# A bias turned by four vector transposes instead of one matrix transpose, in a layernorm, GELU and two-matmul kernel

## The chip, the core and the metric

The kernel runs on one core of a Trainium2 chip. The core has a matrix engine (PE, with its weight loads PEld), a vector engine (DVE), a scalar engine (ACT), a third elementwise engine (POOL) and an engine that issues transfers (SP). Each engine works through its own list of instructions in order and waits on semaphores that other engines and transfers raise. On-chip memory (SBUF) and the accumulation banks (PSUM) have 128 partitions. The metric is the device time of one execution in microseconds (us), less is better.

## What is computed

```python
B, S, D, F = 1, 2048, 1024, 3584          # bf16 inputs
y = layernorm(x)                          # over the last axis, eps 1e-5
h = gelu(y @ w1 + b1)                     # tanh form; b1 has F entries
out = h @ w2 + b2
```

The change touches only how `b1` is brought into the layout in which it is added.

## The kernel before

**Tiles and blocks.** The 2048 rows of x form 16 tiles of 128 rows, in four blocks of 512 (`TB`). The first product is made transposed: one "row" r of 128 columns of w1 times a block gives a 128 x 512 tile of h transposed, in one PSUM bank, by eight matmuls of 128 x 512 (one for each slice dt of D). There are 28 such rows (`FT`). GELU on ACT reads the bank, adds the bias and writes `hT_sb`. The bias must therefore lie with one h column per partition: `b1_sb` is 128 x 28, and row r uses its column r as the per-partition bias (L396 to L399). In memory b1 is a line of 3584 numbers, so it is loaded as 28 rows of 128 (`b1r_sb`) and has to be turned.

**The bias before.** ACT issues the load of b1 and then the load of the first piece of w1, "w0" (`issue`, L216 to L226). `pe_b1` (L520) turns `b1r_sb` with one PE transpose of 28 x 128 into bank "1_1", and `put_b1` (L524) copies it from there to `b1_sb` on ACT. Both stand ahead of all other PE and ACT work except the 25 warm-up matmuls (`warm`, L458) and the first two issues of ACT; the call is at L561. The first matmul that writes bank "1_1" waits for this copy (`bank_read`).

**The start of the first block.** Tiles 0, 1 and half of 2 are turned on PE as they arrive (`pe_T_one`, L326: six slices of tile 0, two of tile 1, two of tile 0, six of tile 1), copied out by ACT (`put_copy`, L336), and multiplied without being normalised ("raw"). Eight rows ("the wave", `R_WAVE`) are open at once in eight PSUM banks, and their matmuls (`pe_wave`, L377) come in the order in which pieces of w1 land. Tile 3 is normalised by DVE and joins last, with 56 + 8 narrow matmuls row by row (L621 to L624).

**The repairs.** Since tiles 0 to 2 went in raw, each wave row is repaired in PSUM on DVE: an operation a (`ops_fix`, L545) that adds the mean's part and an operation b (L548) that multiplies by one over the deviation. GELU of row r on ACT waits for b of row r and for "b1c", the bias copy. In between, DVE makes centred copies of the raw tiles in four operations `ctr0` to `ctr3` (L538): two before the repairs, two after those of the first two rows. The order is written by hand in L628 to L630: a0, a1, b0, b1, ctr2, ctr3, then a and b of rows 2 to 7. DVE's list ends there for the wave; then come scalings of rows 8 to 27 (L412) mixed with the layernorm and the transposes of later blocks, in an order that a planner with estimated due times works out (L668 to L683).

**What waits for the repairs.** Rows 8 to 27 of the first block (`mm1_row`, L404) reuse banks: row 8 takes the bank of row 0, row 9 that of row 1, and so on through five banks, and then row 13 takes the bank "t" of row 7. Each waits for the GELU of the row that held the bank. Rows 8 and up also read the centred tiles, two slices for each `ctr`.

**Other lines.** L469 turns the statistics with transposes of 32 x 96 in groups of four, which step through the 32-partition quarters; L492 and L479 turn half a tile and a whole tile in 32 x 32 blocks, L310 turns later tiles in pieces of 32 x 256; L475 spreads the turned statistics over the partitions (ACT); L608 takes column sums (ACT).

Of the kernel before, what the change touches and what calls it, by code (L numbers as in the profile page):

```python
# [7 lines left out]
BF16 = mybir.dt.bfloat16  # L8
# [4 lines left out]
P = 128  # L13
# [83 lines left out]
def bass_standalone__mixer_channel_mlp__prompt_kernel(  # L97
# [11 lines left out]
    F = w1.shape[1]  # L109
    NT = ST // P  # L110
    DT = D // P
    FT = F // P
# [34 lines left out]
    with ExitStack() as es:  # L147
        sb = lambda name, shape, dt: es.enter_context(nc.sbuf_tensor(name, shape, dt))
# [6 lines left out]
        hT_sb = sb("hT_sb", [P, FT, TB], BF16)  # L155
        o_sb = sb("o_sb", [P, NOB, D], BF16)
        b2_sb = sb("b2_sb", [P, D], BF16)
        b1r_sb = sb("b1r_sb", [FT, P], BF16)
        b1_sb = sb("b1_sb", [P, FT], F32)
        ident = sb("ident", [P, P], BF16)  # L160
        ones = nc.const_aps.tensor(1.0, [P, P], BF16)
# [18 lines left out]
        pe = _Prog("s_pe")  # L180
        act = _Prog("s_act")
# [10 lines left out]
        def dma(dst, src, sig, nbytes, waits=()):  # L192
            dma_q[0].op(lambda e, dst=dst, src=src: e.dma_start(dst, src), waits=waits, sig=sig, sem="d_" + sig, inc=16)
            dma_bytes[0] += nbytes
            est[sig] = DMA_T0 + dma_bytes[0] / DMA_BYTES_PER_US

        def load_x_tile(i):
            dma(x_sb[:, i, :], xf[i * P:(i + 1) * P, :], f"x{i}", P * D * 2)
            x_ev[i] = (f"x{i}", f"x{i}")
# [7 lines left out]
        def load_w1(ci):  # L207
            j0, j1, a, b = w1_chunks[ci]
            dma(w1_sb[:, j0:j1, a:b], w1v[:, j0:j1, a:b], f"w1c{ci}", (j1 - j0) * P * (b - a) * 2)
            w1_issued.add(ci)  # L210
# [5 lines left out]
        def issue(item):  # L216
            if item == "b1":
                dma_q[0] = act
                dma(b1r_sb[:, :], b1.rearrange("(t p) -> t p", p=P), "b1", F * 2)
                dma_q[0] = sp  # L220
            elif item[0] == "x":
                load_x_tile(int(item[1:]))
            elif item[0] == "w" and int(item[1:]) < len(w1_chunks):
                dma_q[0] = act if item == "w0" else sp
                load_w1(int(item[1:]))
                dma_q[0] = sp  # L226

        act.op(lambda e: e.preload_act_table(ACT.Gelu_apprx_tanh))
        for item in SP_FIRST_LOADS:
            issue(item)  # L230
# [8 lines left out]
        for b in range(2, NB):  # L239
# [4 lines left out]
                sig="ident")  # L244
# [70 lines left out]
        def dve_put(o):  # L315
            dve.op(o[0], waits=o[1], sig=o[2])

        pe_t = [T_PE_START]
        bank_read = {}
        bank_of = {"t": ps_t[:, 0, :], "2_0": ps_2b[:, 0, :], "2_1": ps_2b[:, 1, :], "1_1": ps_1b[:, 1, :], "1_2": ps_1b[:, 2, :], "1_3": ps_1b[:, 3, :],  # L320
                   "1_4": ps_1b[:, 4, :]}
# [151 lines left out]
        def put_row_spread(k, q0, q1):  # L473
            for q in range(q0, q1):
                act.op(lambda e, q=q: e.copy(out=row_b(k)[32 * q:32 * (q + 1)], in_=row_b(k)[0:32]),  # L475
                       waits=[f"row_q{k}"], sig=(f"row_{k}" if q == 3 else None))
# [40 lines left out]
                       sig=("te3" if (tq, q) == todo[-1] else None))  # L517
            yT_ev[3] = ["te3"] * DT

        def pe_b1():  # L520
            pe.op(lambda e: e.transpose(out=bank_of["1_1"][:, 0:FT], in_=b1r_sb[:, :], identity=ident[0:FT, 0:FT]),  # L521
                  waits=["ident", "b1"], sig="b1t")

        def put_b1():  # L524
            act.op(lambda e: e.copy(out=b1_sb[:, :], in_=bank_of["1_1"][:, 0:FT]), waits=["b1t"], sig="b1c")
            bank_read["1_1"] = "b1c"

        row_b = lambda k: row_r[:, :, :].rearrange("p (t k) s -> p t k s", k=2)[:, :, k, :]
        raw_cols = lambda bank, c0: unit_bank(bank)[:, c0:c0 + len(RAW) * P].rearrange("p (t s) -> p t s", t=len(RAW))
# [2 lines left out]
        def ops_centre():  # L532
            res = []
            for k, (j0, j1) in enumerate(zip(CENTRE[:-1], CENTRE[1:])):
                xt, ct = [yT_sb[:, k, j0:j1, ycol(RAW[0]):ycol(RAW[0]) + len(RAW) * P].rearrange(
                    "p j (t s) -> p j t s", t=len(RAW)) for k in (0, ybuf(0))]
                m = row_b(0).unsqueeze(1).to_broadcast([P, j1 - j0, len(RAW), P])
                res.append((lambda e, xt=xt, ct=ct, m=m: e.tensor_tensor(out=ct, in0=xt, in1=m, op=ALU.subtract),  # L538
                            ["row_0"], f"ctr{k}", 0.95))
            return res  # L540
# [15 lines left out]
        ctr = ops_centre()  # L556
        seq = st[0] + st[1][:1] + turn_2() + st[1][1:] + st[2] + turn_m[:2] + st[3] + turn_m[2:] + nm[3] + moves_3() + turn_r + ctr[:2]
        for o in seq:
            dve_put(o)

        pe_b1()  # L561
        put_b1()
        T_BANKS = (("t", "2_0"), ("2_1", "1_4"), ("t", "2_0"))
        for t, j in [(0, j) for j in range(N_AHEAD)] + [(1, j) for j in range(GROUPS[1])] + [
                (0, j) for j in range(N_AHEAD, DT)] + [(1, j) for j in range(GROUPS[1], DT)]:
# [40 lines left out]
        def put_cs(c0, c1, src):  # L606
            mine = [r for r in range(R) if c0 <= bank_col(wave[r][0]) < c1]
            act.op(lambda e, c0=c0, c1=c1, src=src: e.mul(ncs[:, c0:c1].unsqueeze(2), src, -1.0),  # L608
                   waits=[f"raw_{r}" for r in mine], sig=f"cs{c0}")
            for r in mine:  # L610
                cs_ev[r] = f"cs{c0}"
# [5 lines left out]
        put_cs(NB1, NB1 + NB2, ps_2[:, 0:NB2, one0:one0 + 1])  # L617
        put_cs(NB1 + NB2, R, ps_tf[:, one0:one0 + 1].unsqueeze(1))
        put_row_spread(1, 3, 4)
        fixes = []  # L620
        for r in range(R):  # L621
            for dt in range(DT):
# [3 lines left out]
            act_gelu(r, 0, TPB, wave[r][0], f"fx_b{r}", f"g_0_{r}")  # L626
            hT_row[(0, r)] = f"g_0_{r}"
        (a0, b0), (a1, b1_) = fixes[:2]  # L628
        for o in [a0, a1, b0, b1_] + ctr[2:] + [o for f in fixes[2:] for o in f]:
            dve_put(o)  # L630
        for t in RAW:
            yT_ev[t] = [f"ctr{k}" for k, (j0, j1) in enumerate(zip(CENTRE[:-1], CENTRE[1:])) for _ in range(j0, j1)]
# [37 lines left out]
        while ci < len(crit) or fi < len(fill):  # L670
# [5 lines left out]
            if take_crit:  # L676
                rdy, o, _ = crit[ci]
                ci += 1
            else:
                rdy, o, _ = fill[fi]  # L680
# [46 lines left out]
```

## Time and profile before

| what | value |
|---|---|
| median of three runs | 396.22 us (395.76 to 396.69) |
| the profiled execution | 396.51 us |
| its span, first to last instruction | 395.3 us |
| granted PE clock, mean | 1.000 |
| PE busy | 390.9 us of the span, 1916 matmuls |
| DVE busy | 162.7 us, 339 instructions |
| ACT busy | 87.1 us, 145 instructions |
| bias load, issue on ACT | 0.81 us, for 0.63 us, 7 KB |
| w0 load, issue on ACT | 1.47 us, for 0.37 us, 128 KB, 3.1 us to landing |
| PE transpose of the bias (L521) | one, 202 ns, at 3.58 us |
| ACT copy of the bias (L525) | one, 182 ns, at 3.82 us |

Times of single instructions are given from the start of the span. A line of the timeline gives start, length, engine, source line, operation, result and operands, shapes and count; instructions of one kind are merged, so that a length can cover several, and in brackets stand the idle time ahead and what ended it. A line of the list of groups gives the count, the busy time, the mean in ns, and the idle time before. Matmuls overlap in their records: the distance between starts is the pace, not the length.

### The profile page before, as it was taken

To read this page: it belongs to the slowest core of one execution; us is meant where nothing else is said; L and a number is where in the kernel's file an instruction comes from. 1 tells how busy PE (TensorE), PEld (TensorE's weight loads), DVE (VectorE), ACT (ScalarE), POOL (GpSimd) and SP (SyncE) were. 2 spreads that over 40 slices of the span, in tenths; PEclk is the share of its full clock that TensorE was granted. 3 is DMA by queue.
4 is the path that set the end of the run, shared out by engine and by line. 5 is a ranking of instruction groups with operands and counts; after the bars stand their busy time and mean duration, and the time that the engine had idled before them with its cause. 6 is when DMAs were issued, how large, how long until landed. Compare 5 with 4: busy or idle time off the path is not lost.

```text
span 395.3 us, 4562 instructions
## 1 busy us (share of the span) xinstructions
PE 390.9 (99%) x1916; PEld 185.8 (47%) x1950; DVE 162.7 (41%) x339; ACT 87.1 (22%) x145; POOL 14.0 (4%) x69
## 2 busy tenths in 40 slices
PE   9999999999999999999999999999999999999998
PEld 8744444444444444444444444444444444444444
DVE  6998889998999306987100000001100000001011
ACT  5655420000134332000023443000003334400000
POOL 5201000011001100000000000000000000000000
PEclk9999999999999999999999999999999999999999
DMA  7999930000000000000000000000000000000000
GB/s 273 375 385 387 387 139 27 15 27 14 28 0 0 2 0 0 28 27 15 27 13 2 0 0 2 13 13 28 25 15 15 0 2 0 0 15 27 13 28 27
DMA packets 16078, 23.63 MB, mean 60 GB/s; under 512 B 1082, under 2 KB 8250, under 8 KB 16058
## 3 DMA queue, kind: packets, MB, share of 16 engines
q1 hardware_dynamic: 15872, 23.20, 16.5%
q8 instruction: 15, 0.25, 0.3%
q10 hardware_dynamic: 186, 0.14, 0.1%
q14 instruction: 5, 0.04, 0.0%
HBM read 19.14 MB, written 4.19 MB: 59 GB/s over the span
## 4 chain that ended last, share of the span: by engine, by line
PE 99%; issue 0%; DVE 0%
PE ps L438 49%; PE ps L370 38%; PE ps_t L370 7%; PE ps L386 3%; PE ps L460 1%; PE ps_t L386 0%; PE ps L331 0%; PE ps_t L331 0%; DVE o_sb L449 0%; PE ps L521 0%
## 5 line engine op out<-in xcount | busy, mean ns | idle before, releaser
L438 PE MATMUL ps<-w_sb,hT_sb 128*128 128x512 bf16 (+2 forms) x909 | 193.3, 373 | 0.8
L370 PE MATMUL ps<-yT_sb,w_sb 128*128 128x512 bf16 x678 | 152.4, 379 | 0.9
L438 PEld LDWEIGHTS ps<-w_sb,hT_sb 128*128 128x128 bf16 x924 | 88.6, 98 | 105.2
L396 ACT ACTIVATE hT_sb<-ps,b_sb 128x512 bf16<-128x512 f32 x94 | 64.0, 688 | 234.9 <-PE ps L370 217.2
L370 PEld LDWEIGHTS ps<-yT_sb,w_sb 128*128 128x128 bf16 x696 | 68.1, 98 | 81.9
L449 DVE TENSOR_TENSOR o_sb<-ps,b_sb 128x512 bf16<-128x512 f32 (+2 forms) x33 | 22.3, 676 | 198.7 <-PE ps L438 198.5
L310 DVE STREAM_TRANSPOSE yT_sb<-x_sb 32x256 bf16<-32x256 bf16 x192 | 83.7, 436 | 21.9 <-PE ps_t L370 18.8
L370 PE MATMUL ps_t<-yT_sb,w_sb 128*128 128x512 bf16 x135 | 31.9, 379 | 0.1
L254 DVE BATCH_NORM_STATS2 st_sb<-x_sb 128x6 f32<-128x512 bf16 x32 | 21.1, 671 | 3.5 <-DMA x_sb<-in_x_dram 3.4
L370 PEld LDWEIGHTS ps_t<-yT_sb,w_sb 128*128 128x128 bf16 x136 | 13.3, 98 | 16.1
L396 ACT ACTIVATE hT_sb<-ps_t,b_sb 128x512 bf16<-128x512 f32 x18 | 12.4, 687 | 17.1 <-PE ps_t L370 14.6
L386 PE MATMUL ps<-yT_sb,w_sb 128*128 128x128 bf16 (+3 forms) x132 | 14.4, 262 | 0.0
L386 PEld LDWEIGHTS ps<-yT_sb,w_sb 128*128 128x128 bf16 x132 | 10.0, 101 | 2.8
L261 POOL TENSOR_TENSOR rstd_sb<-mv_sb,nhalf 128x1 f32<-128x1 f32 x13 | 7.1, 548 | 111.7 <-DVE mv_sb L264 111.7
L412 DVE TENSOR_TENSOR ps<-ps,row_r 128x384 f32<-128x384 f32 x17 | 9.2, 563 | 3.1 <-PE ps L370 2.8
L268 DVE TENSOR_SCALAR x_sb<-x_sb,mv_sb,rstd_sb 128x1024 bf16<-128x1024 bf16 x13 | 7.0, 541 | 2.0 <-POOL rstd_sb L261 1.3
L545 DVE SCALAR_TENSOR_TENSOR ps<-row_r,ncs,ps 128x384 f32<-128x384 f32 x7 | 4.2, 614 | 0.5 <-PE ps L386 0.5
L548 DVE TENSOR_TENSOR ps<-ps,row_r 128x384 f32<-128x384 f32 x7 | 3.9, 563 | 0.2
L538 DVE TENSOR_TENSOR yT_sb<-yT_sb,row_r 128x768 bf16<-128x768 bf16 x4 | 3.6, 952 | 0.0
L460 PE MATMUL ps<-const-bfloat16-1.0 128*128 128x128 bf16 x25 | 2.8, 312 | 0.8 <-PEq L712 0.8
L475 ACT COPY row_r<-row_r 32x384 f32<-32x384 f32 x6 | 3.1, 509 | 2.2 <-DVE row_r L469 2.1
L386 PE MATMUL ps_t<-yT_sb,w_sb 128*128 128x386 bf16 (+1 forms) x16 | 3.2, 273 | 0.0
(37 smaller groups left out, 36.9 us busy)
## 6 DMA issues: line engine op xcount, KB each, us to landing
w_sb<-in_w_dram SPq DMA_DIRECT2D x4, 1792.0 KB, 18.3
w_sb<-in_w_dram SPq DMA_DIRECT2D x2, 2048.0 KB, 15.8
out_dram<-o_sb SPq DMA_DIRECT2D x31, 128.0 KB, 1.7
x_sb<-in_x_dram SPq DMA_DIRECT2D x3, 1024.0 KB, 14.5
w_sb<-in_w_dram SPq DMA_DIRECT2D x7, 256.0 KB, 5.5
x_sb<-in_x_dram SPq DMA_DIRECT2D x4, 256.0 KB, 3.3
w_sb<-in_w_dram SPq DMA_DIRECT2D x1, 1024.0 KB, 9.3
b_sb<-in_b_dram SPq DMA_DIRECT2D x1, 256.0 KB, 14.4
```

Of the source, the lines that this page charges most:

```text
L254: return (lambda e, i=i, h=h, pw=pw: e.bn_stats(st_sb[i][:, 6 * h:6 * (h + 1)], x_sb[:, i, h * pw:(h + 1) * pw]), [x_ev[i][h if len(x_ev[i ...
L261: pool.op(lambda e, i=i, dst=dst, mv=mv: e.tensor_tensor(out=dst, in0=mv[:, 1:2], in1=nhalf[:, i:i + 1], op=ALU.pow), waits=[f"mv{i}", "nh ...
L268: return (lambda e, i=i, c0=c0, c1=c1: e.tensor_scalar(out=x_sb[:, i, c0:c1], in0=x_sb[:, i, c0:c1], scalar1=mv_sb[:, i, 0:1], scalar2=rst ...
L310: res.append((lambda e, src=src, dst=dst: e.transpose(out=dst, in_=src), waits, (f"tr{i}" if lastop else None), 0.47))
L370: pe.op(lambda e, b=b, r=r, dt=dt, bank=bank: e.matmul(unit_bank(bank)[:, 0:TB], lhsT=w1_sb[:, dt, r * P:(r + 1) * P], rhs=yT_sb[:, ybuf(b ...
L386: pe.op(lambda e: e.matmul(unit_bank(bank)[:, n0:n1], lhsT=w1_sb[:, dt, r * P:(r + 1) * P], rhs=yT_sb[:, 0 if tiles[0] in RAW else ybuf(0) ...
L396: act.op(lambda e, r=r, n0=n0, n1=n1, bank=bank: e.activation(out=hT_sb[:, r, n0:n1], in_=unit_bank(bank)[:, n0:n1], func=ACT.Gelu_apprx_tanh,
L412: crit.append((est[sig], (lambda e, reg=reg: e.tensor_tensor(out=reg, in0=reg, in1=row_b(1), op=ALU.mult), [sig, "row_1"], ready, 0.57), 0))
L438: pe.op(lambda e, sl=sl, ft=ft, c0=c0, c1=c1, bank=bank: e.matmul(ps_2[:, bank, 0:c1 - c0], lhsT=hT_sb[:, ft, sl * P:(sl + 1) * P], rhs=w2 ...
L449: crit.append((est[sig], (lambda e, ob=ob, c0=c0, c1=c1, bank=bank: e.tensor_tensor(out=o_sb[:, ob, c0:c1], in0=ps_2[:, bank, 0:c1 - c0], ...
L460: pe.op(lambda e: e.matmul(ps_1[:, 0, 0:P], lhsT=ones, rhs=ones, start=True, stop=True))
L545: return [(lambda e: e.scalar_tensor_tensor(out=reg, in0=row_b(0), scalar=ncs[:, c:c + 1], in1=reg, op0=ALU.mult, op1=ALU.add), [f"m1_0_{r ...
```

## The change

The bias is loaded into 32 rows instead of 28; rows 28 to 31 receive the first four rows of b1 a second time, by a small transfer of their own (1 KB) that ACT issues after w0. Four DVE transposes of 32 x 32 turn it into `b1t_sb` (128 x 32): the q-th takes columns 32q to 32q+31 and writes partitions 32q to 32q+31. They stand in DVE's list in front of a0. The ACT copy to `b1_sb` reads `b1t_sb` in SBUF instead of a PSUM bank, and stands behind the last spreading of the statistics (`put_row_spread(1, 3, 4)`, L619) instead of at the front. The PE transpose is gone, and with it the wait of bank "1_1".

```diff
-        b1r_sb = sb("b1r_sb", [FT, P], BF16)
+        b1r_sb = sb("b1r_sb", [32, P], BF16)
+        b1t_sb = sb("b1t_sb", [P, 32], BF16)
...
-                dma(b1r_sb[:, :], b1.rearrange("(t p) -> t p", p=P), "b1", F * 2)
+                dma(b1r_sb[0:FT, :], b1.rearrange("(t p) -> t p", p=P), "b1", F * 2)
...
                 load_w1(int(item[1:]))
+                if item == "w0":
+                    dma(b1r_sb[FT:32, :], b1[0:(32 - FT) * P].rearrange("(t p) -> t p", p=P), "b1_pad", (32 - FT) * P * 2)
...
-        def pe_b1():
-            pe.op(lambda e: e.transpose(out=bank_of["1_1"][:, 0:FT], in_=b1r_sb[:, :], identity=ident[0:FT, 0:FT]),
-                  waits=["ident", "b1"], sig="b1t")
+        def turn_b1():
+            return [(lambda e, q=q: e.transpose(out=b1t_sb[32 * q:32 * (q + 1), :], in_=b1r_sb[:, 32 * q:32 * (q + 1)]),
+                     ["b1", "b1_pad"], ("b1t" if q == 3 else None), 0.1) for q in range(4)]
 
         def put_b1():
-            act.op(lambda e: e.copy(out=b1_sb[:, :], in_=bank_of["1_1"][:, 0:FT]), waits=["b1t"], sig="b1c")
-            bank_read["1_1"] = "b1c"
+            act.op(lambda e: e.copy(out=b1_sb[:, :], in_=b1t_sb[:, 0:FT]), waits=["b1t"], sig="b1c")
...
-        pe_b1()
-        put_b1()
...
         put_row_spread(1, 3, 4)
+        put_b1()
...
-        for o in [a0, a1, b0, b1_] + ctr[2:] + [o for f in fixes[2:] for o in f]:
+        for o in turn_b1() + [a0, a1, b0, b1_] + ctr[2:] + [o for f in fixes[2:] for o in f]:
             dve_put(o)
```

## The prediction

> **What bounds the kernel now.** I read the busy times first, then the chain of waits that ended last, then the timeline at the two places that the diff touches: the first microseconds, and the stretch from 16.8 us to 29 us where the repairs run.
>
> ```profile
> PE 390.9 (99%) x1916; PEld 185.8 (47%) x1950; DVE 162.7 (41%) x339; ACT 87.1 (22%) x145; POOL 14.0 (4%) x69
> ...
> PE 99%; issue 0%; DVE 0%
> ```
>
> PE is busy for 390.9 of 395.3 us, and the chain is PE from end to end. Single starts of matmuls confirm it: from 3.72 us on, the pace is never broken (a distance twice the usual comes every 10.79 us, which is a missing record). So the time moves by what PE gains or loses. PE work that leaves the head is a gain; a delay elsewhere costs only from where PE has to wait for it.
>
> The head, in the timeline:
>
> ```profile
> 3.43 1.29 DVE L254 BATCH_NORM_STATS2 st_sb<-x_sb 128x6 f32<-128x512 bf16 x2 [3.43 <-DMA x_sb<-in_x_dram]
> 3.58 0.10 PEld L521 LDWEIGHTS ps<-ident,b1r_sb 28*128 28x128 bf16 x1 [0.20 <-issue]
> 3.58 0.20 PE L521 MATMUL ps<-ident,b1r_sb 28*128 28x28 bf16 x1
> ...
> 3.72 0.39 PE L331 MATMUL ps_t<-ident,x_sb 128*128 128x128 bf16 x2
> ```
>
> The last warm-up matmul starts at 3.34 and its kind has a pace of 0.107, so PE could go on at 3.44. The bias transpose starts at 3.58 and tile 0's first transpose at 3.72, though tile 0 was there at 3.43 (DVE starts on it then).
>
> The repairs, on DVE:
>
> ```profile
> 14.97 1.83 DVE L538 TENSOR_TENSOR yT_sb<-yT_sb,row_r 128x768 bf16<-128x768 bf16 x2
> 17.35 1.15 DVE L545 SCALAR_TENSOR_TENSOR ps<-row_r,ncs,ps 128x384 f32<-128x384 f32 x2 [0.54 <-PE ps L386]
> 18.40 1.02 DVE L548 TENSOR_TENSOR ps<-ps,row_r 128x384 f32<-128x384 f32 x2
> 19.34 1.81 DVE L538 TENSOR_TENSOR yT_sb<-yT_sb,row_r 128x768 bf16<-128x768 bf16 x2
> ```
>
> DVE has a hole from 16.80 to 17.35, waiting for tile 3's matmuls of row 0. From 17.35 on it has none until 32.25, so a delay of the first repair reaches all of them. The tightest user of a repair is row 13, which takes the bank of row 7:
>
> ```profile
> 27.92 0.69 ACT L396 ACTIVATE hT_sb<-ps_t,b_sb 128x512 bf16<-128x512 f32 x1 [0.43 <-DVE ps_t L548]
> 28.69 0.53 PEld L370 LDWEIGHTS ps_t<-yT_sb,w_sb 128*128 128x128 bf16 x3
> 28.91 0.59 PE L370 MATMUL ps_t<-yT_sb,w_sb 128*128 128x512 bf16 x2
> ```
>
> GELU of row 7 ends at 28.61, and PE reads the bank from 28.91. With 0.04 us for the handover (DVE's last repair ends at 27.89, ACT starts at 27.92) the slack is 0.26 us. Other users have more: row 8's bank is free at 19.68 and wanted at 20.27; row 10's at 23.01 and 23.7; `ctr3` ends at 21.15 and its first matmul starts at 21.57.
>
> **Removed: the PE transpose.** Without it tile 0's first transpose starts at about 3.45, when tile 0 is there and the last warm-up is through: 3.72 - 3.45 = 0.27 us earlier. But the seventh transpose belongs to tile 1, and before it was made at 4.33 with a weight load that began at 4.29, 0.06 later than its neighbours begin against their matmuls: it was waiting for tile 1's landing. Six transposes from 3.45 at 0.107 end at 4.09; PE then waits until 4.29. What passes is 4.33 - 4.29 = 0.04 us. This stretch runs at the slow pace: 0.107 us for 128 columns until 6.58, 0.056 after it. If the pace changes at the same moment as before, 0.04 us there is 0.02 us later. The gain's ends: 0.02 us, and 0.27 us if tile 1 lands early enough and the change of pace moves along with the work; I take 0.03, since the row of tile 1's weight load is from this very place.
>
> **Removed and moved on ACT.** The copy of the bias (182 ns at 3.82) goes from the front; the next ACT work, at 4.15, waits for PE's transposes, so nothing is gained. Its new place is behind the spreading that ends at 17.60, and ACT is next wanted at 19.00. It reads SBUF now; the nearest row is the 32 x 64 copies of L509 at about 241 ns. Behind it in ACT's list stands every GELU: it costs nothing while the turned bias is there before 18.7, and what it costs later is the lateness itself.
>
> **Added: the transfer.** One more issue on ACT, behind w0's, which ends at 1.84; at 0.37 to 0.63 us it ends by 2.5, and ACT's first wait after that is past 3.9. It moves no SP or POOL issue. Its 1 KB stands beside 271 to 389 KB moved in each us there. It is needed at 16.7; w0, issued in front of it in the same list, took 3.1 us.
>
> **Added: four transposes on DVE.** The trace has none of 32 x 32. Its rows:
>
> ```profile
> L469 DVE STREAM_TRANSPOSE row_r<-stat_r 32x96 f32<-32x96 f32 x8 | 2.1, 267 | 0.2
> ...
> L479 DVE STREAM_TRANSPOSE xq_sb<-x_sb 128x1024 bf16<-128x1024 bf16 x1 | 1.2, 1245 | 0.0
> ...
> L492 DVE STREAM_TRANSPOSE xq_sb<-x_sb 128x512 bf16<-128x512 bf16 x1 | 0.7, 687 | 0.0
> ```
>
> The 256-column ones (L310) take 436 ns on average. From 96 to 256 columns that is 1.06 ns a column, so 32 columns take 267 - 64 x 1.06 = 199 ns. The line through 512 and 1024 columns (1.09 ns a column) gives 687 - 480 x 1.09 = 164 ns, the low end; the high end is the 32 x 96 row itself, 267 ns. I take 0.20 us, from the two nearest rows.
>
> How they queue matters as much. Two `ctr` together take 1.83 us at 0.95 each, so the second starts 0.08 before the first has ended. Four L469 in a row take 1.11 us at 0.267 each: no overlap, 0.013 between. The new four step through the partition quarters as L469 do. So: start 16.72, end 16.72 + 4 x 0.20 + 3 x 0.013 = 17.56; a0, writing PSUM, may overlap by 0.08 and starts at 17.48, 0.13 after the 17.35 of before. Ends: 16.72 + 4 x 0.164 + 0.04 - 0.08 = 17.34, no delay; without any overlap at 0.267, 16.82 + 4 x 0.267 + 0.05 = 17.94, a delay of 0.59. Then `ctr2`: it overlapped b1 by 0.09 (19.34 against 19.43). The statistics that follow a stepping L469 start 0.01 behind its end, without overlap (8.94, then 8.96), so I give `ctr2` 0.10 more. The delay of row 7's repair is 0.23 us (0.10 to 0.69).
>
> [...]
>
> **The sum.** PE arrives at row 13 0.03 earlier, at 28.88; the bank is ready at 28.61 + 0.23 + 0.04 = 28.88. Hence no stall, and at most 0.03 us gained: 396.51 - 0.03 = 396.5 for the profiled execution. That execution lies 0.29 above the median of the runs, so on the median's scale the forecast is 396.2, no change. The bounds: -0.27 with the full gain and the short transposes, 395.95; 0.69 - 0.26 = +0.43 with the long ones, 396.65.
>
> **Rivals.**
>
> *The head's gain passes whole* (0.14). For it: 0.27 us of PE time leaves. Against: tile 1's weight load at 4.29, and a row 13 that takes back any gain beyond what the repairs allow. It gives -0.13 (full gain at the changed pace) to -0.27: 396.0.
>
> *DVE overruns its hole* (0.12). Place: between `ctr1` and a0; it decides from the point where row 7's repair is later than 0.26 us, that is transposes above about 0.21 us each. At 0.267 without overlap the price is +0.43: 396.65, slower. For it: L469 has no overlap and no smaller transpose is in the trace. Against: the price must fall with columns, as 1245, 687, 436 do.
>
> *The change of pace comes later* (0.07). PE's pause of 0.2 us before tile 1 stands nearer to 6.58 than the pauses of before (3.44 to 3.72). The faster pace came 5.75 us after PE's first matmul at 0.83; if the count began anew at 4.29 it would come at 10.04, 3.46 us later, and the loss is 3.46 x (1 - 56/107) = 1.65: 397.9. Against: the pauses of before began no such count, for 3.72 + 5.75 would be 9.47. [...]
>
> *The pad is late, and the transposes stand still* (0.03): the change would then not do what it says. The slowest loads of the page need 18.3 us to land; issued by 2.3, the pad would come at 20.6, DVE would lose 3.9 us more than its slack, and the time is 400.1. Against: those are 1792 KB.
>
> **How the numbers follow.** The forecast has 0.64. A measurement of this kernel can tell about 0.2%, 0.79 us, from no change; the runs of before spread from -0.46 to +0.47. Faster by more: 0.07 of the forecast's share, 0.42 of the first rival's and 0.05 of the second's, 0.11. Slower by more: 0.07 of the forecast's share, 0.02 of the first rival's, a quarter of the second's, 0.8 of the third's, all of the fourth's, 0.17. The rest, 0.72, is within. The range takes both bounds and the spread of runs: 395.95 - 0.46 = 395.5 to 396.65 + 0.47 = 397.1.
>
> **What will show it.** Tile 0's first transpose near 3.45 and a pause of PE before 4.29; the full pace again near 6.58; four DVE transposes of about 0.20 us from 16.7, the first repair near 17.48, `ctr2` not overlapping; GELU of row 7 ending near 28.84 and row 13's matmuls starting near 28.9. The forecast is wrong if a transpose takes 0.27 or more, if PE pauses at row 13, or if the pace changes at another time.

## The result, and the profile after

The kernel after takes 396.80 us (median of 20 runs, 396.47 to 397.35), the kernel before 396.14 us (median of 20 runs, 395.70 to 396.76). The ratio is 1.0017, 95% interval 1.0010 to 1.0023: 0.66 us slower. The interval lies clear of 1, so the loss is real, though it is just under the 0.2% that the prediction took as the least that a measurement can tell. The profiled execution after takes 396.83 us, with a span of 395.6 us against 395.3.

The chain of waits of the kernel after has changed its kind. Below, the first line gives the busy times; of the last two, which are the chain, one gives shares by engine and one by engine and source line (the diff moves L538 to L540, L545 to L547, L548 to L550, L370 to L373; the new transposes are L524):

```profile
PE 392.6 (99%) x1949; PEld 185.1 (47%) x1949; DVE 163.4 (41%) x343; ACT 87.0 (22%) x145; POOL 14.1 (4%) x69
...
PE 94%; DVE 3%; DMA 1%; issue 1%; SPq 0%; POOL 0%
PE ps L441 49%; PE ps L373 38%; PE ps_t L373 7%; DMA x_sb<-in_x_dram 1%; DVE st_sb L257 1%; DVE yT_sb L540 1%; DVE xq_sb L482 0%; DVE row_r L472 0%; DVE ps L547 0%; DVE ps L550 0%; SPq L194 0%; DVE yT_sb L490 0%; DVE b1t_sb L524 0%; POOL rstd_sb L264 0%; DVE x_sb L271 0%
```

Before, the chain was PE from end to end. Now it leaves PE in the first block and goes back through DVE: the repairs, the new transposes (`b1t_sb L524`), the centring, the statistics, and the landing of x. PE's busy share is still 99%, so this part of the page alone would not have told it.

DVE's timeline around the change, in the kernel after:

```profile
15.25 1.83 DVE L540 TENSOR_TENSOR yT_sb<-yT_sb,row_r 128x768 bf16<-128x768 bf16 x2
17.00 0.84 DVE L524 STREAM_TRANSPOSE b1t_sb<-b1r_sb 32x32 bf16<-32x32 bf16 x4
17.77 1.09 DVE L547 SCALAR_TENSOR_TENSOR ps<-row_r,ncs,ps 128x384 f32<-128x384 f32 x2
18.78 1.01 DVE L550 TENSOR_TENSOR ps<-ps,row_r 128x384 f32<-128x384 f32 x2
19.83 1.83 DVE L540 TENSOR_TENSOR yT_sb<-yT_sb,row_r 128x768 bf16<-128x768 bf16 x2
```

There is no hole: centring, four transposes and first repair run into one another, and the bracket that named PE as the releaser of the first repair is gone. The first repair starts at 17.77 instead of 17.35, and `ctr2` at 19.83 instead of 19.34.

What PE and its weight loads waited for between 19 and 30 us, in the kernel after (total us, times, longest):

```profile
PEld ps L373 <- DVE yT_sb L540: 0.8, 2, 0.6
PEld ps_t L373 <- ACT hT_sb L399: 0.4, 1, 0.4
...
PEld ps L373 <- ACT hT_sb L399: 0.4, 1, 0.4
PE ps L373 <- ACT hT_sb L399: 0.2, 1, 0.2
```

The same question to the kernel before named no wait of PE there. By the starts of single matmuls PE loses 0.38 us before row 8 (GELU of row 0), 0.30 at the seventh slice of row 8 (`ctr3`), and 0.11 before row 13 (GELU of row 7): 0.79 in all, 0.13 more than the change costs in the median. In the profiled pair the loss shows as only 0.29 us of span, because PE was ready for row 8 at 19.73 us in this execution and at 20.27 in the one before.

### The profile page after: what moved, and what is told of

Its sections match the earlier page's. It is cut to its first block, busy times and chain, and to the rows that moved or that the text cites. A ratio compares the mean times of both kernels' runs of the same rounds, so it can differ in the third digit from the quotient of the medians.

```text
span 395.6 us, 4600 instructions
## 1 busy us (share of the span) xinstructions
PE 392.6 (99%) x1949; PEld 185.1 (47%) x1949; DVE 163.4 (41%) x343; ACT 87.0 (22%) x145; POOL 14.1 (4%) x69
## 4 chain that ended last, share of the span: by engine, by line
PE 94%; DVE 3%; DMA 1%; issue 1%; SPq 0%; POOL 0%
PE ps L441 49%; PE ps L373 38%; PE ps_t L373 7%; DMA x_sb<-in_x_dram 1%; DVE st_sb L257 1%; DVE yT_sb L540 1%; DVE xq_sb L482 0%; DVE row_r L472 0%; DVE ps L547 0%; DVE ps L550 0%; SPq L194 0%; DVE yT_sb L490 0%; DVE b1t_sb L524 0%; POOL rstd_sb L264 0%; DVE x_sb L271 0%
## 5 line engine op out<-in xcount | busy, mean ns | idle before, releaser
L373 PE MATMUL ps<-yT_sb,w_sb 128*128 128x512 bf16 x696 | 153.7, 379 | 0.4 <-ACT hT_sb L399 0.2
L373 PEld LDWEIGHTS ps<-yT_sb,w_sb 128*128 128x128 bf16 x696 | 67.9, 98 | 82.7 <-DVE yT_sb L540 0.8
L373 PE MATMUL ps_t<-yT_sb,w_sb 128*128 128x512 bf16 x136 | 32.1, 379 | 0.0
L373 PEld LDWEIGHTS ps_t<-yT_sb,w_sb 128*128 128x128 bf16 x136 | 13.2, 98 | 16.2 <-ACT hT_sb L399 0.4
L547 DVE SCALAR_TENSOR_TENSOR ps<-row_r,ncs,ps 128x384 f32<-128x384 f32 x7 | 4.2, 605 | 0.0
L550 DVE TENSOR_TENSOR ps<-ps,row_r 128x384 f32<-128x384 f32 x7 | 3.8, 560 | 0.2
L540 DVE TENSOR_TENSOR yT_sb<-yT_sb,row_r 128x768 bf16<-128x768 bf16 x4 | 3.7, 955 | 0.1
```

The costliest lines, as they stand in the source:

```text
L373: pe.op(lambda e, b=b, r=r, dt=dt, bank=bank: e.matmul(unit_bank(bank)[:, 0:TB], lhsT=w1_sb[:, dt, r * P:(r + 1) * P], rhs=yT_sb[:, ybuf(b ...
L547: return [(lambda e: e.scalar_tensor_tensor(out=reg, in0=row_b(0), scalar=ncs[:, c:c + 1], in1=reg, op0=ALU.mult, op1=ALU.add), [f"m1_0_{r ...
```

## The experiments

Each kernel was timed in turn with the kernel before on the same chip; e5 was profiled only. A is the theory that DVE's list, lengthened by the four transposes, sets the end of the first block; B that the second load delays tile 2 and with it DVE; C that PE's pace rises at another time without the PE transpose.

**e1, the four transposes taken out of the kernel after.**

```diff
         def turn_b1():
-            return [(lambda e, q=q: e.transpose(...), ...) for q in range(4)]
+            return []
...
+        pool.op(lambda e: e.memset(b1t_sb[:, :], 0.0), sig="b1t")
...
-            act.op(lambda e: e.copy(out=b1_sb[:, :], in_=b1t_sb[:, 0:FT]), waits=["b1t"], sig="b1c")
+            act.op(lambda e: e.copy(out=b1_sb[:, :], in_=b1t_sb[:, 0:FT]), waits=["b1t", "b1", "b1_pad"], sig="b1c")
```

> The kernel after without the four DVE transposes; the second load of four rows, the missing PE transpose and the late ACT copy stay. The bias is left out (zeros are added). Theory A (DVE's list is the limit of the first block, and the four transposes lengthen it): the first repair starts as soon as PE allows, ctr2 overlaps b1 again, PE does not pause at row 8, at ctr3 or at row 13, and the time is that of before or up to 0.3 us less. Theory B (the second load delays tile 2 and with it DVE): the transpose of tile 2 still starts at about 5.7 instead of 5.45, and the time is 0.2 to 0.3 us above before. Theory C (without the PE transpose the pace of PE rises at another time): the pace rises near 5.65 again, not at 6.58.

Measured: 396.18 us against 396.23, ratio 1.0000 (0.9991 to 1.0008). Both loads, the missing PE transpose and the late ACT copy together cost nothing and bring nothing, to within 0.4 us either way. In the profiled execution the first repair waits for PE again and `ctr2` (19.18) starts inside the 1.02 us of the b operations:

```profile
15.06 1.83 DVE L540 TENSOR_TENSOR yT_sb<-yT_sb,row_r 128x768 bf16<-128x768 bf16 x2
17.20 1.15 DVE L547 SCALAR_TENSOR_TENSOR ps<-row_r,ncs,ps 128x384 f32<-128x384 f32 x2 [0.31 <-PE ps L390]
18.25 1.02 DVE L550 TENSOR_TENSOR ps<-ps,row_r 128x384 f32<-128x384 f32 x2
19.18 0.95 DVE L540 TENSOR_TENSOR yT_sb<-yT_sb,row_r 128x768 bf16<-128x768 bf16 x1
```

Against B: the second load is there and the time is that of before; the transpose of tile 2 starts at 5.53, where the profiled execution of after had it at 5.70. Against C as a cause: the PE transpose is missing here as in after, and the loss is gone; the slow pace ends at 4.12, neither near 5.6 nor near 6.58.

**e2, one load of 32 rows instead of two.**

```diff
-                dma(b1r_sb[0:FT, :], b1.rearrange("(t p) -> t p", p=P), "b1", F * 2)
+                dma(b1r_sb[:, :], bass.AP(b1.tensor, b1.offset, [[12 * P, 2], [P, 16], [1, P]]), "b1", 32 * P * 2)
...
-                if item == "w0":
-                    dma(b1r_sb[FT:32, :], ...)
...
-                bias=b1_sb[:, r:r + 1], scale=1.0),
+                bias=b1_sb[:, r + (4 if r >= 16 else 0):r + (5 if r >= 16 else 1)], scale=1.0),
...
```

> The kernel after with one load instead of two: 32 rows, namely rows 0 to 15 and rows 12 to 27 of the bias, and GELU takes column r or r + 4. Nothing else changes. Theory A: the time stays at +0.5 to +0.8 us against before. Theory B: tile 2 lands at about 5.26 again, DVE is 0.25 to 0.4 us earlier, and the time is +0.2 to +0.4 us.

Measured: 398.58 us, ratio 1.0054 (1.0035 to 1.0073). Neither theory expected this, and the time does not tell them apart, because the new load is not the old one with four rows more. In ACT's list of issues it takes 1.24 us to issue and pushes w0 back:

```profile
0.83 1.24 ACTq L194 DMA_DIRECT2D b1r_sb<-in_b_dram  x1
2.10 0.36 ACTq L194 DMA_DIRECT2D w_sb<-in_w_dram  x1
```

In the kernel after the first load takes 0.65 us to issue and w0 follows at 1.49. Here PE pauses for 0.66 us before tile 1 and 0.28 before its first product, and keeps the slow pace until 9.18.

The trace does show one thing about A. PE is so late here that the same four transposes lie in DVE's wait for it, with 0.57 us of the wait left behind them, and from row 8 to row 13 PE loses nothing:

```profile
17.65 0.84 DVE L522 STREAM_TRANSPOSE b1t_sb<-b1r_sb 32x32 bf16<-32x32 bf16 x4
19.07 1.15 DVE L545 SCALAR_TENSOR_TENSOR ps<-row_r,ncs,ps 128x384 f32<-128x384 f32 x2 [0.57 <-PE ps L387]
```

**e3, the kernel before with four more transposes that nobody reads.**

```diff
+        def extra():
+            return [(lambda e, q=q: e.transpose(out=ex_sb[32 * q:32 * (q + 1), :], in_=ident[0:32, 32 * q:32 * (q + 1)]),
+                     ["ident"], None, 0.1) for q in range(4)]
...
-        for o in [a0, a1, b0, b1_] + ctr[2:] + [o for f in fixes[2:] for o in f]:
+        for o in extra() + [a0, a1, b0, b1_] + ctr[2:] + [o for f in fixes[2:] for o in f]:
```

> The kernel before, with its PE transpose of the bias, and four more DVE transposes of 32 x 32 in front of the first repair, whose result nobody reads. Theory A: +0.4 to +0.8 us against before, though neither load nor PE has changed; PE pauses at row 8, at ctr3 or at row 13. Theory B and C: within 0.2 us of before. If the forecast's slack of 0.26 us at row 13 held for every execution, +0.1 us or less.

Measured: 396.80 us against 396.23, ratio 1.0016 (1.0007 to 1.0024). Within the scatter that is the loss of the change (0.57 us against 0.66), with the loads, the PE transpose and the ACT copy of before. DVE's timeline has the shape of the kernel after:

```profile
15.00 1.83 DVE L543 TENSOR_TENSOR yT_sb<-yT_sb,row_r 128x768 bf16<-128x768 bf16 x2
16.75 0.84 DVE L526 STREAM_TRANSPOSE ex_sb<-ident 32x32 bf16<-32x32 bf16 x4
17.52 1.09 DVE L550 SCALAR_TENSOR_TENSOR ps<-row_r,ncs,ps 128x384 f32<-128x384 f32 x2
```

With e1 this settles where the loss is: the transposes on DVE alone make it, and without them there is none.

**e4, one transpose of 32 x 128, on the load of e2.** The one transpose is written as in e8 below.

> One load as in the run with one load, one DVE transpose of 32 x 128 in front of the first repair instead of four of 32 x 32, and four ACT copies that put the quarters on their partitions. On DVE it costs about 0.30 us instead of 0.84, and it ends on the first quarter, so ctr2 may overlap b1 again. Theory A: the time falls by 0.5 to 0.6 us against the run with one load, to -0.1 to +0.25 us against before. Theory B: no difference to the run with one load.

Measured: 398.19 us, ratio 1.0050 (1.0033 to 1.0068). The load of e2 hides what was to be seen: PE waits 1.06 us for w0 and keeps the slow pace until 10.08, and the first repair waits for PE until 19.62. As in e2, DVE has time to spare, and nothing follows for A or B.

**e5, the kernel before once more.**

> The kernel before, unchanged, profiled once more. If the hole in DVE's list ahead of the first repair (0.54 us in the profiled execution of before) belongs to executions in which the pace of PE rises late, then here, with a pace that rises before 6 us, the hole is 0.3 us or less; with one that rises near 6.5 us it is about 0.5 again. If the hole belongs to the kernel, it is 0.54 whatever the pace.

Measured: 395.93 us, span 394.7. The slow pace ended before 4 us, and the hole is not smaller but gone:

```profile
15.12 1.83 DVE L538 TENSOR_TENSOR yT_sb<-yT_sb,row_r 128x768 bf16<-128x768 bf16 x2
16.87 1.14 DVE L545 SCALAR_TENSOR_TENSOR ps<-row_r,ncs,ps 128x384 f32<-128x384 f32 x2
17.92 1.02 DVE L548 TENSOR_TENSOR ps<-ps,row_r 128x384 f32<-128x384 f32 x2
```

The first repair starts at 16.87, before the second `ctr` has ended (16.95), and no releaser is named. At the other end GELU of row 7 is through at 28.12, and row 13's weight load waits 0.2 us for it, until 28.17; its first matmul still starts on time, at 28.29. In this execution the kernel before has only about 0.1 us left at row 13, where the execution that was read had 0.26.

**e6 and e7, eight and two such transposes in the kernel before.** As e3, with `for h in range(2) for q in range(4)` into a tile twice as wide, and with `for q in (1, 0)`.

> The kernel before with eight DVE transposes of 32 x 32 in front of the first repair, twice those of the run with four, results unread. If DVE's list alone sets the end of the first block from the fourth on, the second four cost their whole 0.86 us: +1.3 to +1.6 us against before. If part of the +0.6 is a fixed cost of having such transposes there at all, less than +1.1.

> The kernel before with two DVE transposes of 32 x 32 in front of the first repair, second quarter first, so that the last output is on the first quarter and ctr2 may overlap b1. It adds 0.36 to 0.43 us to DVE's list. With the slack of 0.26 at row 13 and a hole of about 0.05 to 0.1 in the usual execution: +0.1 us (0 to +0.2). If the hole of 0.54 held for all: 0.

Measured: eight, 397.54 us against 396.35, ratio 1.0035 (1.0022 to 1.0048, which is +0.9 to +1.9 us); two, 396.25 us against 396.35, ratio 1.0000 (0.9991 to 1.0010). So the first two are free to within 0.4 us either way, four cost 0.57, eight 1.2 to 1.4: behind the first two the cost grows about as what they add to DVE. Eight came out a little under the expectation by the medians and inside it by the ratio, whose interval also reaches below the +1.1 of the other theory; a fixed cost of more than 0.4 us for having them there is excluded by the run with two. In its profiled execution PE loses 0.21 us between row 8 and row 13, so two are not free in every execution.

e7 also shows the overlap at `ctr2`: its last transpose writes the first quarter, and `ctr2` starts at 19.31, inside b, which ends at 19.38:

```profile
18.37 1.01 DVE L553 TENSOR_TENSOR ps<-ps,row_r 128x384 f32<-128x384 f32 x2
19.31 0.94 DVE L543 TENSOR_TENSOR yT_sb<-yT_sb,row_r 128x768 bf16<-128x768 bf16 x1
```

In the kernel after, where the last transpose writes the last quarter, b ends at 19.79 and `ctr2` starts at 19.83.

**e8, the kernel after with one transpose of 32 x 128 and four ACT copies.**

```diff
-        b1t_sb = sb("b1t_sb", [P, 32], BF16)
+        b1t_sb = sb("b1t_sb", [32, P], BF16)
...
-            return [(lambda e, q=q: e.transpose(...), ["b1", "b1_pad"], ("b1t" if q == 3 else None), 0.1) for q in range(4)]
+            return [(lambda e: e.transpose(out=b1t_sb[:, :], in_=b1r_sb[:, :]), ["b1", "b1_pad"], "b1t", 0.3)]
...
-            act.op(lambda e: e.copy(out=b1_sb[:, :], in_=b1t_sb[:, 0:FT]), waits=["b1t"], sig="b1c")
+            for q in range(4):
+                act.op(lambda e, q=q: e.copy(out=b1_sb[32 * q:32 * (q + 1), :], in_=b1t_sb[:, 32 * q:32 * q + FT]),
+                       waits=["b1t"], sig=("b1c" if q == 3 else None))
```

> The kernel after with its two loads, but one DVE transpose of 32 x 128 in front of the first repair and four ACT copies that put the quarters on their partitions. DVE's list grows by 0.22 to 0.30 us, no overlap is lost at ctr2. If DVE's length is all that the change cost: within 0.15 us of before, 0.5 us under after. If the transposes of DVE are not the cause, +0.6 us as after.

Measured: 396.23 us against 396.35, ratio 0.9999 (0.9990 to 1.0008). The loss is gone, with the same loads and without the PE transpose:

```profile
15.02 1.83 DVE L541 TENSOR_TENSOR yT_sb<-yT_sb,row_r 128x768 bf16<-128x768 bf16 x2
16.76 0.29 DVE L524 STREAM_TRANSPOSE b1t_sb<-b1r_sb 32x128 bf16<-32x128 bf16 x1
17.20 1.15 DVE L548 SCALAR_TENSOR_TENSOR ps<-row_r,ncs,ps 128x384 f32<-128x384 f32 x2
```

One transpose of four blocks takes 0.29 us where four of one block take 0.84. The four ACT copies (0.21 us each) run from 17.48 to 18.37, before GELU of row 0 at 18.85. This form of the change costs nothing that can be measured; it does not beat the kernel before, and e1 says that there was little to win: with no turning at all the time is the same to within 0.4 us.

## Why the prediction was wrong

It forecast no change, 396.2 us, and the kernel is 0.66 us slower. Most of its terms were right:

- *PE bounds the kernel before.* Right for both executions of it that were profiled. In e5 DVE comes close to its limit beside PE, with about 0.1 us left at row 13.
- *Four transposes of 0.20 us, stepping without overlap, 17.56 - 16.72 = 0.84 from the first start to the last end.* Measured: 200 ns on average, 0.84 us. The 32 x 96 row at 267 ns and the 32 x 256 ones at 436 ns, from which the prediction drew its line, gave the right number for 32 columns.
- *`ctr2` loses its overlap, 0.10 us.* Right in kind; in after it starts 0.03 us behind the end of b where it used to start 0.09 before it, 0.12 in all. In the runs it goes with the quarter of the partitions that the last transpose writes: the last quarter in after; the first in e7 and e8, where `ctr2` starts 0.07 us (19.31 against 19.38) and 0.09 (19.19 against 19.28) before the end of b. What makes it so was not shown.
- *The transfer and the ACT copy cost nothing.* Right, by e1, to within 0.4 us. The copy takes 0.21 us at 17.87 and GELU of row 0 starts at 19.36.
- *The slack of 0.26 us at row 13.* Right, and not only in the execution that was read, as shown below. (PE writes that bank from 28.91 on; the prediction says that it reads it.)
- *The head brings 0.03 us.* By e1 it brings nothing that can be measured. Tile 0's first transpose starts at 3.58 in after, not at 3.45: tile 0 landed at 3.45, and 0.13 us pass until PE works on it. PE's pause before tile 1 came in e1 (0.19 us) and e8 (0.17), not in after.

The step that failed is the cover: "DVE has a hole from 16.80 to 17.35, waiting for tile 3's matmuls of row 0". The prediction set the 0.84 us against those 0.54 and was left with a delay of 0.13 for the first repair, where in after the first repair came 0.97 behind what PE allowed. The hole is not a property of the kernel. It is how far DVE is ahead of PE in one execution, and PE's time of arrival there varies. These are PE's narrow matmuls of tile 3 in the execution of before that was read, in e5 and in after; the first eight belong to row 0:

```profile
16.70 3.29 PE L386 MATMUL ps<-yT_sb,w_sb 128*128 128x128 bf16 x56
...
16.09 3.29 PE L386 MATMUL ps<-yT_sb,w_sb 128*128 128x128 bf16 x56
...
16.16 3.29 PE L389 MATMUL ps<-yT_sb,w_sb 128*128 128x128 bf16 x56
```

The next table has all ten traces, in us, from the starts and ends of single instructions. "Row 0" is the start of row 0's last narrow matmul. Where the first repair waited for PE it started 0.26 later (the same in five traces), and "late" is how far behind that it started. "PE loses" is the time from PE's readiness for row 8 (the end of its narrow matmuls) to row 13's first matmul, less the 8.63 that it takes where nothing is in its way.

```
kernel, execution     slow pace ends  second ctr ends  row 0  first repair  late  PE loses
before, the one read            6.58            16.80  17.09         17.35  0.00      0.00
before, e5                before 3.8            16.95  16.48         16.87  0.13      0.00
e1 (no transposes)              4.12            16.88  16.94         17.20  0.00      0.00
e8 (one of 32 x 128)            5.07            16.85  16.94         17.20  0.00      0.00
e7 (two, unread)                4.22            16.98  16.60         17.36  0.50      0.21
e3 (four, unread)               4.76            16.83  16.60         17.52  0.66      0.50
after (four)                    5.57            17.08  16.55         17.77  0.97      0.81
e6 (eight, unread)              6.36            16.94  17.01         18.50  1.24      1.08
e2 (four, late PE)              9.18            17.73  18.81         19.07  0.00      0.00
e4 (one, late PE)              10.08            17.46  19.36         19.62  0.00      0.00
```

In e3 and in after PE released the first repair at about 16.86 and 16.81, when DVE was just done with centring or still at it, and so the transposes had no hole to lie in. The rest of the prediction's sum holds in every trace: the lateness, plus the 0.12 at `ctr2` where the last transpose ends on another quarter, less the slack of 0.26 at row 13, gives 0.24 for e7, 0.52 for e3, 0.83 for after and 1.10 for e6, each within 0.03 of what PE loses. From row 13's first matmul to the end the span is 366.4 us in all ten, so what PE has lost by then is lost for good.

When PE comes to row 0 depends on when its pace rises, but not on that alone: e1 and e8 are late with an early pace, because PE there stood still for a piece of w1 (e1's line is shown at the end), which landed at 7.25 us in both and at 6.47 in e5. How often the kernel before runs with a hole and how often without is not known; two executions of it were profiled, one of each kind.

The execution that was read was also 0.29 us slower than the median. The prediction used that number only to shift its result to the median's scale. It was the warning: what made that execution late, a PE that came late, is the same thing that made its hole. PE was ready for row 8 at 20.27 us there and at 19.66 in e5, 0.61 apart, and the spans, 395.28 and 394.67, differ by as much.

Of the rivals, the overrun of DVE is what happened, at its place and in its mechanism; the prediction made it depend on transposes above 0.21 us, and they were not (0.193 to 0.204). It decided on the length of the hole instead. The later change of pace did not occur in after, where the slow pace ended at 5.57. The pad came in time: the transposes start at 17.00, before centring has ended.

Not settled: tile 2 landed at 5.67 in the profiled execution of after, and its transpose starts at 5.70; in before, e1, e3, e5, e6, e7 and e8 it starts at 5.45 to 5.59. e1 and e8 have the same second load, so it is not that load by itself; that it is the scatter of landings was not shown. By an estimate it makes about 0.2 of the 0.97 in the table, since without the transposes the first repair could have started where the first of them did, at 17.00.

## What to carry to other kernels

Before work is put into a hole of an engine, ask what ends the hole and whether that varies from run to run; a hole that was there because another engine came late (0.54 us of DVE, in the execution that was read) was gone where that engine came early (e5). If the profiled execution lies off the median, its holes may be those of an off execution; a second profile of the unchanged kernel (e5) would have shown it. And four tiny instructions cost nearly three times one of the same work here: one transpose over four blocks did in 0.29 us what four did in 0.84.

## What the runs showed of the hardware that was not expected

The moment at which PE's pace goes from 0.107 to 0.056 us for 128 columns moved between 3.8 us at the latest (e5) and 6.6 us (before) over eight profiled executions of kernels with nearly the same head, with pauses of up to about 0.2 us before it. With pauses of 0.66 (e2) and 1.06 us (e4) among the first matmuls it came only at 9.18 and 10.08; that the pauses did this was not tested. The earliest and the latest of the eight lie at least 2.8 us apart; what sets the moment was not shown.

An early pace is not always kept as time. In e5 the span is 0.61 us shorter than in the execution of before that was read. In e1 the slow pace ended 2.5 us earlier than in that execution, but then PE stood still for a piece of w1 that had not landed, as its timeline shows, and the span was only about 0.15 us shorter:

```profile
6.42 0.44 PE L390 MATMUL ps<-yT_sb,w_sb 128*128 128x128 bf16 x5
7.39 0.49 PE L390 MATMUL ps<-yT_sb,w_sb 128*128 128x386 bf16 x2 [0.52 <-DMA w_sb<-in_w_dram]
```

A load whose source steps in two dimensions over the rows (e2) took 1.24 us to issue for 8 KB (1.23 in e4), the plain one of 7 KB 0.63 (before) and 0.65 (after).
